# Score tiles kept for the whole run: the next products of a pair's first item wait for that item's top-eight alone, with fewer unread products ahead

## The chip, the cores and the metric

The kernel runs on one core of one Trainium2 chip. The metric is the device time of one execution in microseconds (us). Before the change the median of three runs is 797.43 us (797.13 to 797.91).

## The reference

For 8 batches of 8 heads, with 576 positions and a head size of 64, attention keeps only the 32 largest scores of each row. The result goes through a highway layer with two 512 x 512 weights.

```
scores = scale * np.matmul(q, k.transpose(0, 1, 3, 2))
kth = np.partition(scores, -top_k, axis=-1)[..., -top_k:-top_k + 1]
scores = np.where(scores >= kth, scores, -1e9)
attn = np.exp(scores - max);  attn = attn / (sum + 1e-9)
x = matmul(attn, v)                       # heads side by side: (4608, 512)
H = maximum(x @ w_h, 0);  T = sigmoid(x @ w_t + b_t)
out = T * H + (1 - T) * x
```

## The kernel before

**Units and pairs.** The 576 query rows of a head are four tiles of 128 and a short one of 64. A unit (L59 to L65) is one full query tile of one head, or the short tiles of two heads one above the other in the 128 partitions. Two units make a pair: 288 units, 144 pairs, 18 pairs a batch, of which the last two are the short query tile. An item is one of the two units of a pair; the code calls them s = 0 and s = 1.

**The score tile.** `scores` (L297 to L349) writes the products of query and key of one pair into a tile of three PSUM banks. Item 0 takes bank 0 and the first 64 columns of bank 1, item 1 the last 64 columns of bank 1 and bank 2. For a full query tile four f32 products of 64 rows by 256 columns fill banks 0 and 2 (L311); item 0's operands lie in the partitions 0 to 63, item 1's in 64 to 127. The loop over the two column halves is outside, that over the items inside, so the items alternate. One product with a block-diagonal operand fills both ends in bank 1 (L322). For the short tile each item has four products of 64 x 64 (L328) and two for the ends (L339), item 0 first. The tile comes from a pool of two buffers (L81, L299), so that the products of pair i + 2 wait until every reader of pair i's tile is done.

**What happens to a score tile.** For pair i + 1, DVE finds the eight largest of each of the six 96-wide segments of either item (`segments`, L358, twelve instructions), ACT copies both items to SBUF (L353), and DVE combines the segment lists (`refine`, L375 to L391) into the 24th largest value, a threshold. ACT marks what lies above it with a sign and counts it (`mask_count`, L406, one instruction per item, each followed by a read of the sum). PE adds the marks onto the scores in PSUM (`mask_add`, L419, four products), so that the marked values drop, and DVE takes the top-eight of all 576 columns of each item (`below`, L432, two instructions), which gives the values from rank 25 to 32. From these comes the 32nd value (L438, L448, L451). ACT computes the exponentials (L424); the smaller ones are cut off by a comparison on ACT (L454) or POOL (L457) and a minimum on DVE (L471). A DMA transposes the result (L496), PE multiplies it with the values (L509), and ACT copies a full block of four heads' results out (L523).

**The order of a step.** The order on every engine is written out by hand in `step` (L790 to L908), under a manual schedule. In step i PE's queue takes: the mask additions of pair i (L815); work left from the step before (L824); the values of pair i - 3 (L826), and where these fill a block, the copy on ACT; unread products (`spare`, L829); in some steps a transposition of the next batch's keys or queries (L251); the products of pair i + 2 (L844); a layer's projection (L537 to L551) or a transposition; and four or ten more unread products (L853). DVE takes the segments of pair i + 1, `below` of pair i, `refine` of pair i + 1 and the minimum. Each engine works its queue in order.

**Unread products.** `spare(n)` (L275) issues n bf16 products of 128 x 252 columns into the unused part of the value block's tile; nobody reads them. Ahead of the score products stand 8 of them, or 3 where the pair i + 2 is short and the value block is empty. After a block's copy they write the same single buffer, and so wait for that copy.

`finish` (L965) does the last pair, with the last layers, and takes two more score tiles for them; `begin` (L910) takes one ahead of the first pair.

Of the kernel before, what the change touches and what calls it, by code (L numbers as in the profile page):

```python
# [11 lines left out]
FP32 = mybir.dt.float32  # L12
# [14 lines left out]
def kernel(  # L27
# [10 lines left out]
    nc = tc.nc  # L38
    P = nc.NUM_PARTITIONS
# [7 lines left out]
    nfull = S // P  # L47
# [5 lines left out]
    BANK = 512  # L53
    MAIN = nfull * P
# [4 lines left out]
    units = []  # L59
# [7 lines left out]
    pairs = [(u, u + 1) for u in range(0, NU, 2)]  # L67
    NG = len(pairs)
# [9 lines left out]
    xpool = ctx.enter_context(tc.tile_pool(name="x", bufs=3))  # L78
    fpool = ctx.enter_context(tc.tile_pool(name="f", bufs=2))
    hpool = ctx.enter_context(tc.tile_pool(name="h", bufs=3))  # L80
    xps = ctx.enter_context(tc.tile_pool(name="xps", bufs=2, space=bass.MemoryType.PSUM))  # L81
    ops = ctx.enter_context(tc.tile_pool(name="ops", bufs=1, space=bass.MemoryType.PSUM))
    fps = ctx.enter_context(tc.tile_pool(name="fps", bufs=1, space=bass.MemoryType.PSUM))


    ident_f = consts.tile([P, P], FP32)
# [188 lines left out]
    def spare(n):  # L275
        if "t" not in po:
            po.update(t=pso_tile(), n=0)
        for _ in range(n):
            nc.tensor.matmul(  # L279
                po["t"][:, 4 * DE : BANK],  # L280
                ident_b[:],
                cst[:, 0 : BANK - 4 * DE],
                start=True,
                stop=True,
                skip_group_check=True,
            )
# [7 lines left out]

    def scores(pair, prep):  # L297
        kT, qT, kd = prep
        ps = xps.tile([P, 3 * BANK], FP32, tag="x", name="xs")  # L299
        heads2 = [units[u][2] for u in pair]  # L300
        qt = units[pair[0]][1]
        qs = qt * P
        MB = 2 * BANK
        rest = []
        RA, RB = BANK, 2 * BANK - rem
        if qt < nfull:
            hp = heads2[0][0] // 2
            for n0 in range(0, MAIN, 256):
                for s, mo in ((0, 0), (1, MB)):
                    r = s * D  # L310
                    mm = nc.tensor.matmul(  # L311
                        ps[:, mo + n0 : mo + n0 + 256],
                        qT[r : r + D, hp, qs : qs + P],
                        kT[r : r + D, hp, n0 : n0 + 256],
                        start=(n0 == 0),
                        stop=True,
                        skip_group_check=True,
                    )
                    if s:
                        rest.append(mm)  # L320
            ends = ps[:, BANK:MB].rearrange("p (a n) -> p a n", n=rem)[:, 0 :: BANK // rem - 1, :]
            rest.append(nc.tensor.matmul(ends, qT[:, hp, qs : qs + P], kd[:, hp, :], start=True, stop=True))  # L322
        else:
            for (mo, ro), hh in zip(((0, RA), (MB, RB)), heads2):
                hp = hh[0] // 2
                for n0 in range(0, MAIN, 256):
                    for r in (0, D):
                        mm = nc.tensor.matmul(  # L328
                            ps[r : r + rem, mo + n0 : mo + n0 + 256],
                            qT[r : r + D, hp, qs : qs + rem],  # L330
                            kT[r : r + D, hp, n0 : n0 + 256],
                            start=(n0 == 0),
                            stop=True,
                            skip_group_check=True,
                        )
                        if mo:
                            rest.append(mm)
                for r in (0, D):
                    mm = nc.tensor.matmul(  # L339
                        ps[r : r + rem, ro : ro + rem],  # L340
                        qT[r : r + D, hp, qs : qs + rem],
                        kd[r : r + D, hp, r : r + rem],
                        start=(mo == 0),
                        stop=True,
                        skip_group_check=True,
                    )
                    rest.append(mm)
        both = bass.AP(tensor=ps.tensor, offset=ps[:].offset, ap=[ps[:].ap[0], [3 * BANK - S, 2], [1, S]])
        return ps[:, 0:S], ps[:, 3 * BANK - S : 3 * BANK], both, rest  # L349
# [79 lines left out]
        return [t[:, s, :] for s in range(2)] + [t]  # L429

    def below(u, ps):
        nc.vector.max(wall[:, u, THR + 1 : KTH], ps)  # L432


    def hits(pair):
# [302 lines left out]
    def start_scores(g):  # L738
        b = units[pairs[g][0]][0]
        for u in pairs[g]:  # L740
            for h in units[u][2]:
                ensure_prep(b, h // 2)
        st[g] = dict(ps=scores(pairs[g], preps[b]), sc=[None, None], et=[None, None], e=[None, None])
        st[g]["seg"] = 0
        st[g]["cand"] = cands[g % len(cands)]

# [43 lines left out]
    def step(i):  # L790
# [34 lines left out]
        if back:  # L825
            back_pv(j)  # L826
            back_xs(j)
            st.pop(j)
        spare(8 if i + 2 >= NG or units[pairs[i + 2][0]][1] < nfull or po["n"] else 3)  # L829
        ev = prep_filler() if to_prep and (i <= SPB or (len(to_prep) > 15 - k_in or len(layers) > 2) and i % 2) else None  # L830
        do_work(nc.gpsimd, 2 * dm if prev and not ps_["one"] else dm)
        segs(i + 1, 2 * NSEG)
        if live:
            below(pr[0], st[i]["ps"][0])
            below(pr[1], st[i]["ps"][1])
        if live:
            st[i]["e"] = pair_tile("e")
            expo(pr[0], st[i]["sc"][0], st[i]["e"][0])
# [71 lines left out]
    def begin():  # L910
        done.update((0, hp, part) for hp in range(NP) for part in range(2))
        done.update(((0, 0, 7), (0, 0, 8)))
        piece = partial(prep_piece, stages[0], preps[0])
        dve = nc.vector.tensor_copy
        spare(21)
        xa = xps.tile([P, 3 * BANK], FP32, tag="x", name="xs")
        ev0 = piece(0, 3)
        ev1 = piece(0, 5, xa, dve)
        ev2 = piece(0, 4, po["t"], dve)
        ev1()  # L920
        ev0()
        ev2()
        piece(0, 2, xa[:, BANK : 2 * BANK], dve)()
        po.clear()
        start_scores(0)
        piece(0, 6, pso_tile())()
        evs = [piece(1, 0), piece(1, 5, pso_tile())]
        for ev in evs:
# [36 lines left out]
    def finish():  # L965
# [41 lines left out]
        cur["e"] = pair_tile("e")  # L1007
        for s, u in enumerate(pr):
            expo(u, cur["sc"][s], cur["e"][s])
        x1 = xps.tile([P, 3 * BANK], FP32, tag="x", name="xs")  # L1010
# [10 lines left out]
        x2 = xps.tile([P, 3 * BANK], FP32, tag="x", name="xs")  # L1021
# [141 lines left out]
```

## Time and profile before

| what | value |
|---|---|
| median of three runs | 797.43 us |
| the profiled execution | 797.43 us |
| its span, first to last instruction | 795.7 us |
| PE, DVE, ACT, POOL busy | 693.0, 767.3, 756.3, 564.8 us |
| unread products (L279) on PE | 1,841 rows, 247.1 us |
| mean granted clock of PE | 0.996 |

A row of the profile names line, engine, operation, what it writes and reads, its shape and count; then its busy time, the mean length of one in ns, and the engine's idle time ahead of it with what ended that. Rows overlap where an engine starts an instruction before the last one has ended: the rows of PE give the length from start to modelled end, and products that follow each other start sooner than that. PE is the matrix engine and PEld its weight loads. In the timeline the columns are start, length of the merged rows, engine, line, operation and count.

### The profile page before, as it was taken

Reading aid. Unit: us, or ns where it says so; the run is one execution under the profiler, and the core shown is the slowest. Engines: PE = TensorE matmul, PEld = TensorE weight load, DVE = VectorE, ACT = ScalarE, POOL = GpSimd, SP = SyncE. Lnnn points to the kernel's source line nnn. Section 1 sums busy time; section 2 is a strip of 40 time slices with the busy share of each in tenths; the row PEclk is TensorE's granted clock in tenths of the full one; section 3 lists DMA queues with packets and bytes.
Section 4 is the critical chain, followed back from the end, with each engine's and each line's share of the span. In section 5 each row is a group of like instructions: output and inputs, shape, how many; then the busy total and the mean of one; then the engine's idle time right before and its main releaser. Section 6 shows DMA issues by size and latency. Waiting matters only on the chain.

```text
span 795.7 us, 20350 instructions
## 1 busy us (share of the span) xinstructions
PE 693.0 (87%) x6459; PEld 494.6 (62%) x6459; DVE 767.3 (96%) x3947; ACT 756.3 (95%) x1401; POOL 564.8 (71%) x750
## 2 busy tenths in 40 slices
PE   8889988888988888888997889888998888988884
PEld 6666766566656666566665666656666666666552
DVE  6999999999999999999999999999999999999996
ACT  5999999999999999999999999999999999999984
POOL 2666867877778767787777876788777787776760
PEclk9999999999999999999999999999999999999998
DMA  6699967976899567987689866898677975565643
GB/s 125 88 136 172 127 125 140 159 127 87 140 157 156 104 99 135 159 136 117 106 146 159 133 110 111 154 154 127 107 129 146 162 118 96 97 113 98 114 85 89
DMA packets 341780, 100.32 MB, mean 126 GB/s; under 512 B 326048, under 2 KB 333856, under 8 KB 341664
## 3 DMA queue, kind: packets, MB, share of 16 engines
q1 hardware_dynamic: 286448, 79.14, 52.6%
q0 software_dynamic: 53536, 19.34, 22.5%
q8 instruction: 53, 0.87, 0.4%
q10 hardware_dynamic: 1680, 0.46, 0.3%
q14 instruction: 63, 0.52, 0.2%
HBM read 31.72 MB, written 9.44 MB: 52 GB/s over the span
## 4 chain that ended last, share of the span: by engine, by line
DVE 46%; ACT 32%; PE 16%; issue 2%; DMA 2%; SPq 0%; POOL 0%; DVEq 0%; ACTq 0%; POOLq 0%
DVE cand L358 16%; DVE wall L432 15%; ACT m L406 9%; ACT e L424 8%; ACT sc L353 6%; DVE ep L471 6%; ACT r L454 4%; PE xs L328 4%; PE fp L537 3%; PE pso L279 3%; PE xs L419 2%; PE xs L311 2%; DMA xT<-xb 2%; ACT xs L523 2%; DVE en L382 1%
## 5 line engine op out<-in xcount | busy, mean ns | idle before, releaser
L358 DVE MAX8 cand<-xs 128x8 f32<-128x96 f32 x1728 | 298.0, 252 | 0.4 <-PE xs L311 0.2
L279 PE MATMUL pso<-cst,ident_b 128*128 128x252 bf16 x1841 | 247.1, 272 | 41.8 <-ACT xs L523 39.7
L457 POOL TENSOR_SCALAR r<-sc,wall 128x576 bf16<-128x576 f32 x135 | 232.5, 1722 | 0.0
L424 ACT ACTIVATE e<-sc,be 128x576 bf16<-128x576 f32 x288 | 227.8, 791 | 0.1
L279 PEld LDWEIGHTS <-ident_b 128*128 128x128 bf16 x1841 | 173.5, 98 | 80.7 <-issue 48.9
L432 DVE MAX8 wall<-xs 128x8 f32<-128x576 f32 x288 | 205.2, 756 | 13.3 <-PE xs L419 12.1
L311 PE MATMUL xs<-kT,qT 64*128 64x256 f32 x1024 | 145.3, 400 | 34.0 <-DVE high L375 26.0
L353 ACT COPY sc<-xs 128x1152 f32<-128x1152 f32 x144 | 161.7, 1123 | 0.2
L311 PEld LDWEIGHTS xs<-kT,qT 64*128 64x128 f32 x1024 | 93.0, 186 | 65.5 <-issue 39.3
L406 ACT ACTIVATE m<-xs,wall 128x576 int8<-128x576 f32 x144 | 108.1, 751 | 9.8 <-DVE wall L391 8.6
L471 DVE TENSOR_TENSOR ep<-e,r 128x1024 bf16<-128x1024 bf16 (+2 forms) x236 | 116.4, 493 | 0.3 <-issue 0.2
L448 POOL TENSOR_TENSOR hit<-hit,wall 128x18 f32<-128x18 f32 x143 | 32.1, 225 | 113.5 <-DVE hit L438 113.5
L419 PE MATMUL xs<-m,ident_b 128*128 128x512 bf16 (+1 forms) x576 | 104.7, 285 | 9.0 <-ACT m L406 6.8
L406 ACT ACTIVATE m<-sc,wall 128x576 int8<-128x576 f32 x144 | 112.5, 781 | 0.0
L454 ACT ACTIVATE r<-sc,be 128x576 bf16<-128x576 f32 x143 | 111.0, 776 | 0.0
L509 PEld LDWEIGHTS <-et 128*128 128x128 bf16 (+1 forms) x1600 | 68.6, 100 | 19.9 <-issue 3.5
L400 POOL TENSOR_TENSOR be<-wall,fac 128x4 f32<-128x4 f32 x144 | 29.0, 201 | 71.9 <-DVE ep L471 52.0
L509 PE MATMUL pso<-vb,et 128*128 128x65 bf16 (+1 forms) x1600 | 74.4, 194 | 1.0 <-DMA et<-ep 1.0
L419 PEld LDWEIGHTS <-ident_b 128*128 128x128 bf16 x576 | 51.1, 98 | 35.5 <-issue 13.9
L322 PEld LDWEIGHTS xs<-kd,qT 128*128 128x128 f32 x256 | 38.1, 188 | 42.5 <-issue 42.1
L322 PE MATMUL xs<-kd,qT 128*128 128x128 f32 x256 | 62.5, 326 | 0.0
L625 POOL TENSOR_TENSOR s<-h,x 128x512 f32<-128x512 f32 (+1 forms) x37 | 42.8, 1157 | 1.0 <-ACT h L624 1.0
(128 smaller groups left out, 1005.8 us busy)
## 6 DMA issues: line engine op xcount, KB each, us to landing
kin<-in_k_dram SPq DMA_DIRECT2D x64, 128.0 KB, 3.2
qin<-in_q_dram SPq DMA_DIRECT2D x62, 128.0 KB, 3.1
out_dram<-s SPq DMA_DIRECT2D x30, 256.0 KB, 3.1
s<-h POOLq DMA_DIRECT2D x29, 256.0 KB, 3.8
xb<-x POOLq DMA_DIRECT2D x30, 128.0 KB, 2.7
vb<-in_v_dram POOLq DMA_DIRECT2D x28, 128.0 KB, 3.9
et<-ep SPq DMA_TRANSPOSE x143, 3.9
vb<-in_v_dram POOLq DMA_DIRECT2D x24, 64.0 KB, 3.0
```

The lines of the kernel that those rows point to most:

```text
L279: nc.tensor.matmul(po["t"][:, 4 * DE : BANK], ident_b[:], cst[:, 0 : BANK - 4 * DE], start=True, stop=True, skip_group_check=True,)
L311: mm = nc.tensor.matmul(ps[:, mo + n0 : mo + n0 + 256], qT[r : r + D, hp, qs : qs + P], kT[r : r + D, hp, n0 : n0 + 256], start=(n0 == 0), ...
L353: nc.scalar.copy(sc[:], both)
L358: ins = nc.vector.max(cand[:, s, :], sc[:, s * SEG : (s + 1) * SEG])
L406: nc.scalar.activation(m1[:].bitcast(I8)[:, 1 : 2 * S : 2], ps, AF.Sign, bias=wall[:, u, THR : THR + 1], scale=ABOVE, accum_out=csum[:, u ...
L419: nc.tensor.matmul(ps[:, s0:s1], ident_b[:], m1[:, s0:s1], start=False, stop=True, skip_group_check=True)
L424: nc.scalar.activation(e, sc, AF.Exp, bias=tb(u), scale=scale)
L432: nc.vector.max(wall[:, u, THR + 1 : KTH], ps)
L454: nc.scalar.activation(r, sc, AF.Relu, bias=eb(u), scale=BIGK)
L457: nc.gpsimd.tensor_scalar(r, sc, kth(u), None, ALU.is_ge)
L471: return nc.vector.tensor_tensor(out[:, :, c0:c1], e[:, :, c0:c1], r[:, :, c0:c1], ALU.min)
L509: nc.tensor.matmul(pso[r0 : r0 + ql, col : col + DE], ets[s][:, c, gi * P2 : gi * P2 + ql], vb[:, h, vc, :], start=(c == 0), stop=(c == nc ...
```

## The change

The two score tiles are allocated once and taken in turn (`xss`), instead of from a pool of two. The pool kept all products of pair i + 2 behind all readers of pair i; with kept tiles the order follows from what each product overwrites. `below` now returns its instruction, and `step` keeps that of item 1; `scores` gets the one of two pairs back and declares that item 0's products do not depend on it. So item 0's products wait for item 0's `below` alone, item 1's and the ends' for item 1's too. In the full tiles the loop over items goes outside: both products of item 0, then both of item 1. In the short tiles the order stays. Ahead of the score products stand 3 unread products in every step but the last ones (8). `begin` and `finish` name the tiles that they took from the pool before.

```diff
-    xps = ctx.enter_context(tc.tile_pool(name="xps", bufs=2, space=bass.MemoryType.PSUM))
+    xps = ctx.enter_context(tc.tile_pool(name="xps", bufs=1, space=bass.MemoryType.PSUM))
+    xss = [xps.tile([P, 3 * BANK], FP32, name=f"xs{i}") for i in range(2)]
...
-    def scores(pair, prep):
+    def scores(pair, prep, other=None):
+        def ahead(mm):
+            if other is not None:
+                tc.declare_no_dep(mm.ins, other.ins, reason="another bank")
+
-        ps = xps.tile([P, 3 * BANK], FP32, tag="x", name="xs")
+        ps = xss[pair[0] // 2 % 2]
...
-            for n0 in range(0, MAIN, 256):
-                for s, mo in ((0, 0), (1, MB)):
+            for s, mo in ((0, 0), (1, MB)):
+                for n0 in range(0, MAIN, 256):
...
                     if s:
                         rest.append(mm)
+                    else:
+                        ahead(mm)
...
                         if mo:
                             rest.append(mm)
+                        else:
+                            ahead(mm)
...
     def below(u, ps):
-        nc.vector.max(wall[:, u, THR + 1 : KTH], ps)
+        return nc.vector.max(wall[:, u, THR + 1 : KTH], ps)
...
-        st[g] = dict(ps=scores(pairs[g], preps[b]), sc=[None, None], et=[None, None], e=[None, None])
+        st[g] = dict(ps=scores(pairs[g], preps[b], st[g - 2]["below"] if g > 1 else None), sc=[None, None], et=[None, None], e=[None, None])
...
-        spare(8 if i + 2 >= NG or units[pairs[i + 2][0]][1] < nfull or po["n"] else 3)
+        spare(8 if i + 2 >= NG else 3)
...
             below(pr[0], st[i]["ps"][0])
-            below(pr[1], st[i]["ps"][1])
+            st[i]["below"] = below(pr[1], st[i]["ps"][1])
```

In `begin` and `finish` the calls for a new tile become `xss[1]`, `xss[i % 2 ^ 1]` and `xss[i % 2]`.

More of the change, by code (lines that the diff above doesn't have):

```diff
@@ L915, in begin @@
         spare(21)
-        xa = xps.tile([P, 3 * BANK], FP32, tag="x", name="xs")
+        xa = xss[1]
         ev0 = piece(0, 3)
@@ L1009, in finish @@
             expo(u, cur["sc"][s], cur["e"][s])
-        x1 = xps.tile([P, 3 * BANK], FP32, tag="x", name="xs")
+        x1 = xss[i % 2 ^ 1]
         project(bank(x1, 1), z["qt"], z["xT"], wt, True)
@@ L1020, in finish @@
         pick_b(pr, hit)
-        x2 = xps.tile([P, 3 * BANK], FP32, tag="x", name="xs")
+        x2 = xss[i % 2]
         cur["et"] = halves(et_tile())
```

## The prediction

> **What bounds the kernel now.** I read the page first: the busy shares, then the costliest groups.
>
> ```profile
> PE 693.0 (87%) x6459; PEld 494.6 (62%) x6459; DVE 767.3 (96%) x3947; ACT 756.3 (95%) x1401; POOL 564.8 (71%) x750
> ```
> ```profile
> L358 DVE MAX8 cand<-xs 128x8 f32<-128x96 f32 x1728 | 298.0, 252 | 0.4 <-PE xs L311 0.2
> L279 PE MATMUL pso<-cst,ident_b 128*128 128x252 bf16 x1841 | 247.1, 272 | 41.8 <-ACT xs L523 39.7
> ...
> L432 DVE MAX8 wall<-xs 128x8 f32<-128x576 f32 x288 | 205.2, 756 | 13.3 <-PE xs L419 12.1
> L311 PE MATMUL xs<-kT,qT 64*128 64x256 f32 x1024 | 145.3, 400 | 34.0 <-DVE high L375 26.0
> ```
>
> DVE is busy for 767.3 of 795.7 us and ACT for 756.3, so either engine bounds most steps and only their idle time can be won. The segment top-eights (L358), which read the score tiles that this change makes ready sooner, wait 0.4 us in the whole run: they are never late. The only DVE wait of size stands ahead of the full top-eight (L432), 13.3 us, and it is for the mask additions on PE (L419). PE's own waits for DVE ahead of the score products (L311, 34.0 us idle) and ahead of the fillers (L279, 41.8 us) cost nothing unless something behind them is late. Next I read the waits of DVE and of ACT, each by itself.
>
> ```profile
> DVE wall L432 <- PE xs L419: 12.1, 25, 1.1
> ```
> ```profile
> ACT m L406 <- DVE wall L391: 8.6, 23, 0.9
> ACT xs L523 <- PE pso L509: 6.8, 12, 1.1
> ```
>
> So PE holds DVE up 25 times and ACT (the copy of a value block, L523) 12 times. Where? The last two pairs of each batch, the short query tile, are eight places; the waits in a window around the first of them and around the last are these (DVE, ACT, DVE, ACT):
>
> ```profile
> DVE wall L432 <- PE xs L419: 1.1, 2, 0.7
> ```
> ```profile
> ACT xs L523 <- PE pso L509: 0.5, 1, 0.5
> ```
> ```profile
> DVE wall L432 <- PE xs L419: 0.7, 1, 0.7
> DVE wall L432 <- PE pso L509: 0.7, 1, 0.7
> ```
> ```profile
> ACT m L406 <- DVE wall L391: 0.9, 1, 0.9
> ACT xs L523 <- PE pso L509: 0.6, 1, 0.6
> ```
>
> Over the eight windows DVE waits 8.0 us for L419 (six of 1.1, two of 0.7), two thirds of 12.1, and ACT waits 4.6 us for L509 (two of 0.5, six of 0.6). The timeline of PE in the fourth of them shows why.
>
> ```profile
> 376.05 0.48 PE L279 MATMUL pso<-cst,ident_b 128*128 128x252 bf16 x3 [0.70 <-ACT xs L523]
> 376.71 1.08 PE L328 MATMUL xs<-kT,qT 64*64 64x256 f32 x8 [0.17 <-DVE wall L432]
> ...
> 380.92 1.02 PE L279 MATMUL pso<-cst,ident_b 128*128 128x252 bf16 x8
> 381.78 0.60 PE L251 MATMUL fp<-ident_f,qin 128*128 128x128 f32 x4
> 382.46 1.08 PE L328 MATMUL xs<-kT,qT 64*64 64x256 f32 x8
> ...
> 384.56 1.04 PE L537 MATMUL fp<-wt,xT 128*128 128x512 bf16 x4
> ...
> 386.08 0.65 PE L419 MATMUL xs<-m,ident_b 128*128 128x512 bf16 x4
> ```
> ```profile
> 380.88 1.43 DVE L432 MAX8 wall<-xs 128x8 f32<-128x576 f32 x2 [0.35 <-PE xs L419]
> ...
> 386.84 1.43 DVE L432 MAX8 wall<-xs 128x8 f32<-128x576 f32 x2 [0.72 <-PE xs L419]
> ```
> ```profile
> 384.97 0.32 ACT L406 ACTIVATION_READ_ACCUMULATOR m<-sc,wall 128x1 f32 x1
> ...
> 387.09 0.38 ACT L523 COPY xs<-pso 128x260 f32<-128x260 f32 x1 [0.64 <-PE pso L509]
> ```
>
> From 376.71 to 386.57 PE shows no wait at all: eight fillers at 380.92, a transposition, the score products of the second short pair at 382.46, a projection, fillers, and the mask additions at 386.08, though the masks are ready when ACT reads its second sum, at 384.97 + 0.32 = 385.29. PE is the bound here; DVE loses 0.35 and then 0.72, ACT 0.64.
>
> **The change part by part.** *Fillers, 8 to 3.* They go ahead of every pair's products but the last two and those that had 3 already: 1,171 unread products are built instead of 1,841, so 670, or 134 times five. One costs PE (1.02 - 0.27) / 7 = 0.107 us, by the row of 380.92 (first start to last start, one product's 0.27 off), five 0.54 us, and all 72 us. In an ordinary step this is hidden:
>
> ```profile
> 301.99 1.02 PE L279 MATMUL pso<-cst,ident_b 128*128 128x252 bf16 x8 [0.46 <-ACT xs L523]
> 302.94 1.13 PE L311 MATMUL xs<-kT,qT 64*128 64x256 f32 x8
> 304.00 0.49 PE L322 MATMUL xs<-kd,qT 128*128 128x128 f32 x2
> 304.33 1.24 PE L279 MATMUL pso<-cst,ident_b 128*128 128x252 bf16 x10
> 305.40 0.82 PE L419 MATMUL xs<-m,ident_b 128*128 128x512 bf16 x4
> ```
> ```profile
> 301.32 1.43 DVE L432 MAX8 wall<-xs 128x8 f32<-128x576 f32 x2
> ```
>
> Here the products may begin when the second L432 ends, 301.32 + 1.43 = 302.75, and they begin at 302.94; without five fillers PE would reach them at 302.40 and wait.
>
> *The start, item by item.* Item 0's two products (four passes on PE) now wait for the first L432 only. The second starts 1.43 - 0.76 = 0.67 us after the first, so item 0 can start 0.67 us sooner. Item 1's products wait for the second L432 as the whole block did, and the product of the key ends (L322) stands behind them. In the ordinary step item 1 thus starts at 302.75 at the earliest instead of 302.94, the block ends at most 0.19 us sooner, and behind it nothing was late: L358 never waits and the L432 of this step shows no idle time. Worth: 0. For the short pairs the order within an item is unchanged, and the second item's products stand behind the first's, so the whole block moves up with its start.
>
> *The order, item 0 first, then item 1.* Before, the products of the two items alternate. Each f32 product is two passes (1,024 rows at L311 for 128 pairs of four products). Three narrow cuts of PE's timeline through one block:
>
> ```profile
> 302.94 0.49 PE L311 MATMUL xs<-kT,qT 64*128 64x256 f32 x2
> ```
> ```profile
> 303.26 0.38 PE L311 MATMUL xs<-kT,qT 64*128 64x256 f32 x2
> ```
> ```profile
> 303.48 0.38 PE L311 MATMUL xs<-kT,qT 64*128 64x256 f32 x2
> ```
>
> Passes come in pairs that run together, 0.22 us apart. Two passes of one product use the same 64 rows of the array; so the pair at 302.94 is item 0's first pass and item 1's first, and item 1's did not wait for item 0's second, which stands ahead of it in the program. The two halves of the array run as two streams. I take it that this holds in the new order too: item 1's stream starts when its wait ends, whatever remains of item 0's. Cost 0. The bounds: if nothing overlaps, eight passes at 0.22 take 1.76 instead of 0.88, 0.88 us more for each of 128 blocks, of which the earlier start takes back 0.67 or the fillers 0.54. The nearest row, the pair of passes, says 0.
>
> The Trainium skill, "TensorE: Matmul & The Clock Gate", Part 3, says that matmuls stay in program order, "strict FIFO, no reordering". By that rule item 1 would stand behind item 0's four passes, and the time would be that of the first rival below. The pair at 302.94 speaks against it.
>
> *The new sign from the first L432.* DVE now tells PE once more per pair, 142 times. Between 0 and the row's own rounding, 0.02 us each: 0 to 2.8 us; I take 0. The instructions on DVE, ACT, POOL and SP and their order are as before; the static tiles take the turns that the pool gave, so no other wait is added.
>
> *The sum.* In the window of 376 to 387 the first short block starts 0.17 us sooner (PE's idle time there was for L432); it has three fillers before and after. The second gets this and five fillers, 0.17 + 0.54 = 0.71 us: it starts at 381.75, and the first L432 has ended by then, at 380.88 + 0.76 - 0.17 = 381.47. That takes ACT's 0.64 whole and DVE's 0.72 but for 0.01; the additions come at 385.37, just behind the masks' 385.29. What counts is the smaller, ACT's. Over eight batches 4.6 us. DVE is then some 0.1 us ahead of ACT (0.72 and part of 0.35 against 0.64), and wins part of it back where ACT waits for DVE (8.6 us at L406): 8 times 0.06, 0.5 us. In the last batch DVE waits twice 0.7 us: 0.5 us more. The other 12.1 - 8.0 = 4.1 us of L432's waits hold some that hang on a DMA for a projection:
>
> ```profile
> PE fp L537 <- DMA xT<-xb: 2.6, 3, 1.1
> ```
>
> Three, of up to 1.1 us, which nothing here moves: 2.6 us stay at most, and of the 1.5 left I count a third, where fillers made PE late: 0.5 us. Sum 4.6 + 0.5 + 0.5 + 0.5 = 6.1 us. The profiled execution took 797.43 us, 1.7 of it around the span, and that is also the median of the three runs. Forecast **791.3 us**; with every small term at nothing 792.8, with DVE's 8.0 us taken whole and the 1.5 too 787.9.
>
> **Rivals.** *Strict order on PE (slower).* Item 1 runs behind item 0's four passes: in a block gated by L432 the end comes 0.88 - 0.67 = 0.21 us later, in one gated by fillers 0.34. It decides where the mask additions come from PE just in time; ACT's masks hold them up in only 26 of 144 steps:
>
> ```profile
> PE xs L419 <- ACT m L406: 6.8, 26, 0.7
> ```
>
> In the other 118, PE's arrival sets them; with cover in half (the step at 305.40 has 0.3 us), 59 x 0.21 = 12.4 us are lost. The point is 6.1 / 0.21 = 29 exposed steps: above it the change loses. Time 797.4 - 6.1 + 12.4 = 803.7. Chance 0.06.
>
> *The clock falls (slower).* Fillers keep PE busy, and the granted clock is 1.00 in the cuts of the middle:
>
> ```profile
> 182.00:185.50 3.50, 2.27 (x24) 1.34 (x21) 3.50 (x16) 3.50 (x9) 3.13 (x3) 1.00 0.91 134
> 300.00:312.00 12.00, 10.59 (x101) 7.40 (x100) 11.76 (x63) 11.47 (x22) 8.46 (x11) 1.00 0.87 136
> ```
>
> A step takes 795.7 / 144 = 5.5 us. An ordinary stretch is busy for 0.88 and would be for about 0.78 (0.54 us less a step); the emptiest is at 0.65 and could go to 0.50, which no row shows at a full clock. If the clock halved once a batch for a step, PE's 0.78 x 5.5 = 4.3 us would take 8.6, 3.1 more than the step has: 8 x 3.1 = 25 us, 816. Chance 0.04.
>
> *ACT takes over.* ACT is busy for 95%. If its masks hold the additions of the freed step up (they are ready only 0.08 us ahead of the 385.37 above), or if its work, not DVE's, sets the steps after, a quarter of the 6.1 us is won, 1.5: 796.0. Chance 0.14.
>
> *More than the sum.* Ordinary steps with small hidden waits for PE gain as well, up to the 787.9 above: 788.5. Chance 0.12.
>
> *The forecast*, 791.3, between 789.5 and 794: chance 0.64. That the change does not do what it says I leave at nothing: in the built program item 0's first product waits for one DVE sign less than item 1's.
>
> **The numbers.** A measurement of this kernel can tell about 0.2%, 1.6 us, from no change. The range runs from 788.5, the larger gain, to 796.0, where ACT takes over; the two slower rivals, 0.10, and the outer tails of the others are left out. Faster by over 0.2%: 0.64 + 0.12 + 0.05 of ACT's case = 0.81; within: 0.09 of it; slower: 0.06 + 0.04 = 0.10.
>
> **What would show it.** Right: at the short pairs L432's wait falls from 1.1 us a batch to below 0.4, and ACT's at L523 from 0.6 to near 0; L279 has 1,171 rows; item 0's products begin within 0.2 us of the first L432's end, and item 1's passes run beside what is left of item 0's or at the second L432's end; L358 still shows no wait. Wrong: L311's block gets longer by 0.4 us or more counted from the second L432's end, waits at L419 in ordinary steps grow, the granted clock shows under 1.00 before 780 us, or ACT's wait at L406 grows by what L523 loses.

## The result, and the profile after

The changed kernel took 787.9 us (median of four runs, 787.44 to 789.91) beside 797.63 us for the kernel before (four runs); the ratio is 0.9881, with a 95% interval of 0.9867 to 0.9895. It is faster, as forecast, but by 9.7 us instead of 6.1. Eleven later runs of the same kernel (below) took 788.6 to 793.4; the median of all fifteen is 790.35 us. So two questions were open: what made the gain larger than the sum, and why the same kernel differs by 6 us (787.4 to 793.4) from run to run.

The profiled execution took 787.89 us, its span is 786.2 us, the mean granted clock 0.996. First the page: busy shares and groups, with busy time, mean ns, idle time ahead and what ended it.

```profile
PE 683.7 (87%) x5709; PEld 481.4 (61%) x5789; DVE 764.9 (97%) x3947; ACT 753.2 (96%) x1401; POOL 565.8 (72%) x750
...
L316 PE MATMUL xs<-kT,qT 64*128 64x256 f32 x1024 | 209.1, 402 | 21.3 <-DVE wall L441 18.9
...
L441 DVE MAX8 wall<-xs 128x8 f32<-128x576 f32 x288 | 203.8, 747 | 6.3 <-PE xs L428 2.8
...
L280 PE MATMUL pso<-cst,ident_b 128*128 128x252 bf16 x1171 | 174.7, 273 | 43.0 <-ACT xs L532 40.7
```

1,171 unread products (L280) cost 174.7 us, 72.4 less, and PE still holds its share, since the score products (L316) now begin early and wait for the second top-eight within their block. The full top-eight (L441, then L432) has 6.3 us of idle time ahead of it in place of 13.3. The waits of the trace (engine and line waited for, us, times, longest):

```profile
PE xs L428 <- ACT m L415: 15.6, 59, 0.7
...
DVE wall L441 <- PE xs L428: 2.8, 6, 0.9
...
ACT xs L532 <- PE pso L518: 2.2, 4, 1.1
```

DVE's wait for the mask additions fell from 12.1 to 2.8, ACT's for the value block from 6.8 to 2.2, and PE now waits for the masks 59 times instead of 26: at most of the short pairs PE is no longer the late one. The fifth batch's short pairs show it. Before, on PE, on DVE and on ACT (start, length):

```profile
472.97 1.08 PE L328 MATMUL xs<-kT,qT 64*64 64x256 f32 x8 [0.40 <-DVE wall L432]
...
477.19 1.02 PE L279 MATMUL pso<-cst,ident_b 128*128 128x252 bf16 x8
...
478.72 1.08 PE L328 MATMUL xs<-kT,qT 64*64 64x256 f32 x8
...
482.34 0.65 PE L419 MATMUL xs<-m,ident_b 128*128 128x512 bf16 x4
```
```profile
477.14 1.43 DVE L432 MAX8 wall<-xs 128x8 f32<-128x576 f32 x2 [0.35 <-PE xs L419]
...
483.10 1.43 DVE L432 MAX8 wall<-xs 128x8 f32<-128x576 f32 x2 [0.72 <-PE xs L419]
```
```profile
471.66 0.38 ACT L523 COPY xs<-pso 128x260 f32<-128x260 f32 x1
...
477.56 1.13 ACT L353 COPY sc<-xs 128x1152 f32<-128x1152 f32 x1
478.68 0.59 ACT L252 COPY qT<-fp 128x512 f32<-128x512 f32 x1
...
481.32 0.76 ACT L454 ACTIVATE r<-sc,be 128x576 bf16<-128x576 f32 x1
482.11 0.60 ACT L648 ACTIVATE tt<-fp 128x512 f32<-128x512 f32 x1
483.35 0.38 ACT L523 COPY xs<-pso 128x260 f32<-128x260 f32 x1 [0.64 <-PE pso L509]
```

The same place in the changed kernel, again PE, DVE, ACT:

```profile
471.31 0.48 PE L280 MATMUL pso<-cst,ident_b 128*128 128x252 bf16 x3
...
472.26 1.08 PE L335 MATMUL xs<-kT,qT 64*64 64x256 f32 x8
...
475.88 0.65 PE L428 MATMUL xs<-m,ident_b 128*128 128x512 bf16 x4
```
```profile
471.30 1.41 DVE L441 MAX8 wall<-xs 128x8 f32<-128x576 f32 x2
476.64 1.43 DVE L441 MAX8 wall<-xs 128x8 f32<-128x576 f32 x2
481.80 1.41 DVE L441 MAX8 wall<-xs 128x8 f32<-128x576 f32 x2
```
```profile
466.25 0.38 ACT L532 COPY xs<-pso 128x260 f32<-128x260 f32 x1
...
472.16 1.13 ACT L362 COPY sc<-xs 128x1152 f32<-128x1152 f32 x1
473.15 0.62 ACT L253 COPY qT<-fp 128x512 f32<-128x512 f32 x1
...
475.79 0.81 ACT L463 ACTIVATE r<-sc,be 128x576 bf16<-128x576 f32 x1
476.45 0.63 ACT L657 ACTIVATE tt<-fp 128x512 f32<-128x512 f32 x1
476.93 0.41 ACT L532 COPY xs<-pso 128x260 f32<-128x260 f32 x1
```

No wait is left on DVE or ACT. From the first short pair's full top-eight to the second's it was 483.10 - 477.14 = 5.96 us and is 476.64 - 471.30 = 5.34. From one value block's copy to the next ACT took 483.35 - 471.66 = 11.69 us and takes 476.93 - 466.25 = 10.68: 1.01 less, though its idle column had shown 0.64.

Laying the two profiled executions side by side, by the start of each step's segment top-eights (L358, L367), the gain of 9.44 us (their ends included) falls into four parts:

| part | gain, us |
|---|---|
| eight places with the short pairs: 0.42, 1.09, 0.73, 0.73, 1.06, 1.07, 1.06, 0.80 | 6.96 |
| ordinary steps between them, net | 1.38 |
| before the first step | 0.43 |
| behind the last step | 0.67 |

### The profile page after: what moved, and what is told of

It is laid out like the page before. It is cut to its first block, busy times and chain, and to the rows that moved or that the text cites. A ratio compares the mean times of both kernels' runs of the same rounds, so it can differ in the third digit from the quotient of the medians.

```text
span 786.2 us, 18861 instructions
## 1 busy us (share of the span) xinstructions
PE 683.7 (87%) x5709; PEld 481.4 (61%) x5789; DVE 764.9 (97%) x3947; ACT 753.2 (96%) x1401; POOL 565.8 (72%) x750
## 3 DMA queue, kind: packets, MB, share of 16 engines
HBM read 31.72 MB, written 9.44 MB: 52 GB/s over the span
## 4 chain that ended last, share of the span: by engine, by line
DVE 43%; ACT 41%; PE 11%; issue 3%; DMA 2%; SPq 0%; POOL 0%; another core or an unknown queue 0%; DVEq 0%; ACTq 0%; POOLq 0%
DVE cand L367 15%; ACT m L415 12%; DVE wall L441 12%; ACT e L433 10%; ACT sc L362 8%; DVE ep L480 6%; ACT r L463 5%; PE pso L280 2%; PE xs L335 2%; DMA xT<-xb 2%; PE fp L546 2%; DVE en L391 2%; DVE en L394 1%; ACT xs L532 1%; ACT kT L253 1%
## 5 line engine op out<-in xcount | busy, mean ns | idle before, releaser
L367 DVE MAX8 cand<-xs 128x8 f32<-128x96 f32 x1728 | 297.4, 246 | 0.3 <-PE xs L316 0.2
L433 ACT ACTIVATE e<-sc,be 128x576 bf16<-128x576 f32 x288 | 230.6, 801 | 0.1
L316 PE MATMUL xs<-kT,qT 64*128 64x256 f32 x1024 | 209.1, 402 | 21.3 <-DVE wall L441 18.9
L280 PE MATMUL pso<-cst,ident_b 128*128 128x252 bf16 x1171 | 174.7, 273 | 43.0 <-ACT xs L532 40.7
L441 DVE MAX8 wall<-xs 128x8 f32<-128x576 f32 x288 | 203.8, 747 | 6.3 <-PE xs L428 2.8
L316 PEld LDWEIGHTS xs<-kT,qT 64*128 64x128 f32 x1024 | 146.6, 186 | 61.8 <-DVE wall L441 40.6
L280 PEld LDWEIGHTS <-ident_b 128*128 128x128 bf16 x1171 | 108.1, 98 | 75.0 <-issue 49.8
L428 PE MATMUL xs<-m,ident_b 128*128 128x64 bf16 (+1 forms) x522 | 97.5, 275 | 16.9 <-ACT m L415 15.6
L428 PEld LDWEIGHTS <-ident_b 128*128 128x128 bf16 x576 | 53.0, 97 | 47.3 <-issue 25.0
```

Of the source, the lines that this page charges most:

```text
L280: nc.tensor.matmul(po["t"][:, 4 * DE : BANK], ident_b[:], cst[:, 0 : BANK - 4 * DE], start=True, stop=True, skip_group_check=True,)
L316: mm = nc.tensor.matmul(ps[:, mo + n0 : mo + n0 + 256], qT[r : r + D, hp, qs : qs + P], kT[r : r + D, hp, n0 : n0 + 256], start=(n0 == 0), ...
L367: ins = nc.vector.max(cand[:, s, :], sc[:, s * SEG : (s + 1) * SEG])
L428: nc.tensor.matmul(ps[:, s0:s1], ident_b[:], m1[:, s0:s1], start=False, stop=True, skip_group_check=True)
L433: nc.scalar.activation(e, sc, AF.Exp, bias=tb(u), scale=scale)
L441: return nc.vector.max(wall[:, u, THR + 1 : KTH], ps)
```

## The experiments

Ratios stand against runs of the kernel before on the same chip, whose medians were 797.77, 798.01, 797.78 and 797.53 us in the four groups of runs. Gains of single steps are worked out as in the table.

### Which part of the change does it

**Fewer unread products alone.** The kernel before, with 8 -> 3.

```diff
-        spare(8 if i + 2 >= NG or units[pairs[i + 2][0]][1] < nfull or po["n"] else 3)
+        spare(8 if i + 2 >= NG else 3)
```

> The kernel before with 3 unread products ahead instead of 8, nothing else. Theory W (the gain is made where PE alone sets the end, at the two short pairs of each batch, and there the start behind the first top-eight and the five fillers each free PE only as far as the other allows): in the trace of before the second short pair's products start 0.15 us after the second top-eight's end, as do those of most steps, so with the old wait five fillers less free almost nothing there; about 796.5, between 795.5 and 797.2. Rival F (PE's time is what counts, so 5 x 0.107 us less per step do it alone): 788 to 790. Rival S (the earlier start alone does it): 797.6.

Measured: 796.52 us (795.72 to 803.06), ratio 0.9998 (0.9981 to 1.0015). Neither short pair gained more than 0.06 us in any batch. Without an earlier start PE reaches the products sooner and then waits for the second top-eight. The other steps of the profile gained 1.4 us, as with the whole change, and the median is 1.25 us lower than before; three of the twelve runs, at a mean clock of 0.988 to 0.991, took 799 to 803 us and bring the ratio, which is one of means, to 1.

**The early start alone.** The changed kernel with the old line for the unread products.

> The changed kernel with the 8 unread products of before: only the start item by item and the order are new. Theory W: the first short pair of a batch starts 0.1 to 0.6 us sooner, since it has 3 fillers in both, and the top-eight after it loses its wait of 0.35 us (0.46 with the overlap of 0.09 that it usually has); the second short pair keeps its wait of 0.72 us, since PE works without a gap from the first to it. About 795, between 794 and 796. Rival F: 797.6. Rival S: 788 to 789.

Measured: 795.17 us (793.93 to 795.49), ratio 0.9961 (0.9949 to 0.9974). In most batches the first short pair gained 0.12 to 0.46, as with the whole change, and the second 0.07 to 0.16 (0.50 to 0.62 with the whole change); in the third batch the second gained 0.52 of 0.73. The eight places together gained 3.5 us. With eight products in the way PE reaches the second pair's block late whatever may start early.

**The early start in the short pairs alone**, with three unread products:

```diff
                     if s:
                         rest.append(mm)
-                    else:
-                        ahead(mm)
```

> The changed kernel, but in the full query tiles item 0's products wait for both top-eights again; in the short tiles they wait for item 0's alone. Theory W: the full tiles' early start is worth nothing by itself, as item 1's products and the ends' set the block's end; 787.9 to 788.9. Rival S (the early start counts in all steps, 126 of 142 are full): 7/8 of the gain is lost, 796. Rival F: 787.9.

Measured: 791.26 us (788.29 to 794.75), ratio 0.9923 (0.9899 to 0.9948). The short pairs gained as with the whole change, step by step within 0.04.

**The early start in the full tiles alone**, the same cut in the other branch.

> The changed kernel, but in the short tiles item 0's products wait for both top-eights again, and only the full tiles start early. Theory W: the short pairs lose what the early start gives there, up to 0.6 us at the first and up to 0.6 at the second, most of a gain of 0.7 to 1.1 us a batch; 794 to 796. Rival S: 789. Rival F: 787.9.

Measured: 796.15 us (793.91 to 799.97), ratio 0.9972 (0.996 to 0.9984); the first short pair gained nothing, the second 0.10 in most batches and the last batch 0.35, 1.0 us in all.

So the 7 us need two things at once and at one place: the start by item and at most three unread products, both at the short pairs. Apart they bring 0.2 and 3.5 us there. In full tiles the early start is worth nothing that can be measured.

### Which engine sets the freed steps

The prediction counted what ACT showed as idle, the smaller of two figures. Two loads test it: one copy of 128x512, read by nobody, in the step behind the short pairs of every batch, once on ACT and once on DVE.

```diff
             copy_both(i + 1)
+        if k_in == 16:
+            nc.scalar.copy(idle_o[:], idle_i[:])
```

> The changed kernel with one more ACT copy of 128x512 f32 (0.6 us, some 0.5 from start to start) in each of the eight batches, in the step in which ACT stood idle for 0.64 us ahead of L523, behind the score copy; its result isn't read. Theory W (DVE's work sets the steps, ACT lags and catches up in ordinary steps, where its instructions take about 0.6 us less than DVE's): the time grows by 0 to 1.5 us, 788 to 789.5. Rival A, the prediction's own (ACT's idle time caps what a batch gains): 8 x 0.5 = 4 us, 792.

Measured: 794.09 us (792.51 to 800.23), ratio 0.997 (0.9952 to 0.9988), 3.1 us above the changed kernel on the same chip. ACT and DVE of this run in the fifth batch:

```profile
482.28 0.68 ACT L851 COPY idle_o<-idle_i 128x512 f32<-128x512 f32 x1
482.80 0.83 ACT L433 ACTIVATE e<-sc,be 128x576 bf16<-128x576 f32 x1
```
```profile
480.06 1.43 DVE L441 MAX8 wall<-xs 128x8 f32<-128x576 f32 x2
485.66 1.43 DVE L441 MAX8 wall<-xs 128x8 f32<-128x576 f32 x2 [0.36 <-PE xs L428]
```

The copy takes 0.52 us of ACT (482.28 to 482.80), and six of the eight batches lost 0.47 to 0.51 us by it (the fourth 0.22, the last nothing). DVE's next full top-eight comes 5.60 us after the last one instead of 5.16, and waits, since the masks are late. ACT has no room here.

The same copy on DVE (`nc.vector.tensor_copy`):

> The changed kernel with one copy of 128x512 on DVE, read by nobody, in the step behind the two short pairs of each batch, where the same copy on ACT cost its whole 0.48 us a batch. Theory ACT (ACT alone sets these steps, DVE has the 0.4 us to spare that it waited more than ACT): nothing to 0.15 us a batch, the time of the changed kernel within 1 us. Rival both (DVE and ACT had lost the same 1.0 us a batch to the late additions, ACT part of it hidden in the overlap of its rows): most of the copy, 0.25 us or more a batch, 2 us or more in all.

Measured: 792.02 us (790.26 to 794.45), ratio 0.9929 (0.9911 to 0.9946), 1.25 us above the changed kernel on the same chip. DVE in the fifth batch:

```profile
480.86 1.43 DVE L441 MAX8 wall<-xs 128x8 f32<-128x576 f32 x2
482.21 0.41 DVE L851 COPY idle_o<-idle_i 128x512 f32<-128x512 f32 x1
486.35 1.41 DVE L441 MAX8 wall<-xs 128x8 f32<-128x576 f32 x2
```

From top-eight to top-eight it is 5.49 us instead of 5.16: 0.33 is lost, all that the copy holds DVE for (its next row starts at 482.53, 0.32 later). So it is in six batches, 0.33 or 0.34; the fourth lost 0.08. So DVE has no room either, and the reading by which it had 0.4 us to spare falls: both engines had lost the same to the late additions. The total rose by less than the 2 us expected; in the profile later steps give a part back: three that lose 0.25, 0.31 and 0.33 us in the changed kernel lose nothing in this run.

The fourth batch is the exception in both runs: there ACT and DVE each had 0.25 us to spare. A run below without unread products at this place shows who held it up.

### Why the changed kernel's time differs from run to run

**The changed kernel again**, twice, on two more chips.

> The changed kernel as it is, once more beside the three others. Each theory expects 787.9, and steps in which a projection waits for a DMA to come and go by up to 1 us from run to run.

Measured: 791.03 us (788.58 to 793.4), ratio 0.9919 (0.9906 to 0.9933).

> The changed kernel as it is, a third time. Theory clock (its runs differ by the number of 3.4 us stretches at half clock that they happen to get): time falls as the granted clock rises, runs at 0.996 take 787.4 to 788.5 us, each 0.001 less adds about 1 us, median 788 to 791.5. Rival (the spread comes from elsewhere, transfers above all): no relation between clock and time among the runs.

Measured: 790.77 us (789.08 to 793.43), ratio 0.9913 (0.9897 to 0.993). The profiled run took 792.39, 4.5 us more than the first profile, and at the short pairs it gained the same to within 0.02 us. What differs is 3.76 us in the first five steps, 1.34 us in step 81 and, the other way, 0.79 us in step 117. Of the 3.76, 2.14 are lost ahead of the first step. PE's timeline there, in this run and in the first profile:

```profile
7.07 0.66 PE L252 MATMUL fp<-ident_f,kin 128*128 128x128 f32 x2 [0.64 <-DMA kin<-in_k_dram]
...
9.23 1.84 PE L316 MATMUL xs<-kT,qT 64*128 64x256 f32 x8
```
```profile
6.07 0.41 PE L252 MATMUL fp<-ident_f,kin 128*128 128x128 f32 x2
...
7.83 1.13 PE L316 MATMUL xs<-kT,qT 64*128 64x256 f32 x8
```

The first load comes 1.0 us later, and the same block of eight products takes 1.84 us instead of 1.13. The clock had not risen yet: the trace's record of the full clock begins at 10.71 us in this run and at 5.68 in the first profile, and the next such block, at 13.10, takes 1.14. The other 1.62 us are a fall of the clock. Stretches of both runs (bounds and length, busy time of PE, PEld, DVE, ACT, POOL, then the granted clock, the DMA share and GB/s):

```profile
21.00:24.30 3.30, 1.55 (x13) 1.15 (x14) 2.98 (x17) 3.30 (x6) 2.14 (x3) 1.00 0.35 22
24.50:27.70 3.20, 3.20 (x16) 2.05 (x13) 2.43 (x13) 2.84 (x7) 2.60 (x3) 0.50 0.99 117
```
```profile
19.40:22.70 3.30, 1.64 (x15) 1.19 (x13) 3.22 (x15) 3.30 (x6) 2.14 (x4) 1.00 0.22 18
22.80:26.10 3.30, 2.97 (x24) 2.37 (x24) 3.15 (x14) 3.30 (x7) 2.17 (x3) 1.00 1.09 139
```

PE was busy for 1.55 of 3.30 us and then had half its clock for 3.4 us: its two steps lost 1.78 us, where the first profile lost 0.16, with 1.64 of 3.30 at the same place and the clock kept. The difference in step 81 is a transfer. PE waits for it in the profile of before and in this run, and not at all in the first profile of the changed kernel, which waits at another place:

```profile
433.17 1.04 PE L537 MATMUL fp<-wh,xT 128*128 128x512 bf16 x4 [1.14 <-DMA xT<-xb]
```
```profile
433.08 1.04 PE L546 MATMUL fp<-wh,xT 128*128 128x512 bf16 x4 [1.44 <-DMA xT<-xb]
```
```profile
616.80 1.04 PE L546 MATMUL fp<-wh,xT 128*128 128x512 bf16 x4 [1.21 <-DMA xT<-xb]
```

So the expectation that clock alone makes the spread is half right. In this group the two runs at clock 0.997 were the shortest (789.08 and 789.5), but the four at 0.993 to 0.995 lie between 790.51 and 793.43 without order. Over more runs the link is plainer. Of all fifteen runs of the changed kernel the five at 0.996 or 0.997 took 787.4 to 789.5 us, the ten below 788.6 to 793.4. Of the twelve with fewer unread products alone, nine at 0.993 or above took 795.7 to 797.6 and the three below 799.1 to 803.1.

### What the unread products are for

**None ahead of the score products**, `spare(8 if i + 2 >= NG else 0)`:

> The changed kernel with no unread products ahead of the score products at all, instead of 3. Theory W: at the short pairs PE is 3 x 0.107 us sooner, and the first short pair no longer waits for ACT's copy L532; of the 0.13 + 0.14 us that DVE still waits there (0.22 each with the overlap) up to 0.2 each are won, 0 to 3 us in all, 785 to 788; ACT's masks are ready only 0.15 to 0.24 us before the additions then, which caps it. Rival C (the fillers hold the clock): the granted clock falls below 0.99 and the time is above 790.

Measured: 797.25 us (793.36 to 803.86), ratio 0.9998 (0.9977 to 1.0019), mean clock 0.984 in the profile and 0.966 to 0.984 over the runs. All of the gain is gone, though in the profile the short pairs gain 6.97 us as before: the other steps lose 6.32. Six stretches of 3.4 us ran at half clock, and the steps at each lost 0.9 to 1.7 us against the first profile; one from the middle, and the stretch ahead of it:

```profile
417.90:421.20 3.30, 2.39 (x19) 1.70 (x15) 3.30 (x18) 3.30 (x7) 2.52 (x4) 1.00 0.89 157
421.40:424.60 3.20, 2.93 (x22) 1.87 (x21) 2.78 (x15) 3.16 (x8) 3.17 (x4) 0.50 1.03 127
```

**None around the short pairs alone**, three elsewhere:

```diff
+        spare(8 if i + 2 >= NG else 0 if k_in in (14, 15, 16) else 3)
...
+        spare(0 if k_in in (14, 15) else 4 if late else 10)
```

> The changed kernel without any unread products in the steps that issue the two short pairs' products, none ahead of them (nor in the step behind) and none ahead of the next mask additions; the other steps keep 3 and 4 or 10. Theory W: like the one without fillers ahead, and 4 x 0.107 us more at the additions, but ACT's masks cap it at some 0.2 us for each of 16 pairs: 785 to 787.5. Rival C: as above. Rival F: 8 x 2 x 0.43 to 0.75 = 7 to 12 us less, 776 to 781.

Measured: 792.38 us (790.5 to 794.3), ratio 0.9927 (0.9913 to 0.9942). In the fifth to seventh batch the pairs gained 0.45 and 0.77 and lost 0.11 in the next step, so there PE's last 0.1 us is not the limit any more. In the fourth they gained 0.45 and 0.45, 0.17 more than with the changed kernel, and lost nothing behind: there PE still was the late one, which is why a load on ACT or DVE cost less. Three stretches ran at half clock, and the total is 1.35 us above the changed kernel's on the same chip.

**None in the steps at all**, neither there nor ahead of the mask additions:

> The changed kernel with no unread products in the steps at all, neither ahead of the score products nor ahead of the mask additions (those of the start, the finish and the last two steps stay). Theory clock (fillers earn their place by holding the granted clock): the clock falls in many stretches of 3.4 us, mean granted clock below 0.98, and with 0.6 to 1.2 us lost in each the time is above 797 us. Rival (fillers are dead weight on PE, the clock needs few of them): clock above 0.99 and 788 us or less.

Measured: 821.01 us (814.58 to 826.29), ratio 1.0283 (1.0245 to 1.032). A long stretch of this run and of the first profile:

```profile
60.00:420.00 360.00, 297.19 (x2095) 196.34 (x2093) 344.39 (x1777) 343.26 (x637) 262.56 (x341) 0.88 0.77 128
```
```profile
60.00:420.00 360.00, 318.06 (x2673) 223.05 (x2710) 356.10 (x1845) 355.13 (x663) 274.17 (x355) 1.00 0.81 134
```

With the fillers gone the clock is 0.88 in place of 1.00 (0.865 over the run), PE does less in the same time, and DVE and ACT lose some 12 us each in this stretch alone (344.39 and 343.26 busy of 360, against 356.10 and 355.13). The unread products pay for themselves by the clock.

**Eight in full tiles, three at the short pairs.** If only the short pairs gain, the other fillers could stay and hold the clock:

```diff
+        spare(8 if i + 2 >= NG or units[pairs[i + 2][0]][1] < nfull else 3)
```

> The changed kernel, with eight unread products again ahead of the products of full tiles and three only ahead of the two short pairs of each batch. Theory S (all of the gain sits at the short pairs, where the start by item and the five fillers fewer are both needed; the other 500 or so fillers that the change left out cost nothing where they stood, and hold the clock up): 788 to 790 us, as fast as the changed kernel's quick runs, its runs within about 2 us of each other, granted clock 0.996 or more in the profile and no stretch below 1.00 before 770 us. Theory F (eight fillers in the way of full tiles cost time also in ordinary steps): 792 to 795 us.

Measured: 791.84 us (790.16 to 792.73), ratio 0.9923 (0.991 to 0.9936): between the two theories, and both have a share. This version has 630 more unread products than the changed kernel. The short pairs gained as before but for 0.26 us in the second batch, the clock stayed full up to 774.6 us, and the five runs differ by 2.6 us (4.8 and 4.4 in the two repetitions above). But two steps with a projection lost 0.96 and 0.60 us, which lost 0.10 and nothing with three products, several others were 0.1 to 0.3 longer than with three, and the finish is 2.0 us longer. In the two steps and in the finish PE waits for a transfer (the second step's wait is 0.54 us), here and, in the finish, in the first profile:

```profile
235.61 1.04 PE L546 MATMUL fp<-wh,xT 128*128 128x512 bf16 x4 [1.07 <-DMA xT<-xb]
...
773.95 0.89 PE L518 MATMUL pso<-vb,et 128*64 128x65 bf16 x20 [2.11 <-DMA et<-ep]
```
```profile
770.98 0.83 PE L518 MATMUL pso<-vb,et 128*64 128x65 bf16 x20 [1.06 <-DMA et<-ep]
```

So the fillers' own price is the 0.1 to 0.3 of some steps. The larger losses stand at waits for transfers, and they are not the luck of one run: the profiles of the next two versions, also with eight, wait at the same places (0.58 and 0.72 us, 0.53 and 0.56 us, in the finish 2.42 and 2.26), while the changed kernel waits in neither step in any of its three profiles, and 1.02 to 1.06 us in the finish. In turn all three versions miss the wait of 1.0 to 1.3 us at 307 to 311 us that the changed kernel's profiles have. How the products move these transfers is not shown. Two variants of it: the early start only at the short pairs, and the items alternating again in full tiles.

> As the run with eight fillers in full tiles, but item 0 starts behind its own top-eight in the short pairs alone; in full tiles all products wait for the second full top-eight. Theory S: within 1 us of that run, since the early start in full tiles hides no wait. Rival (the early start in full tiles is worth something, in the steps where a projection stands ahead of the mask additions): 1.5 to 3 us slower.

Measured: 792.26 us (789.72 to 793.08), ratio 0.9924 (0.9911 to 0.9936).

> As the run with eight fillers in full tiles, but the products of the two items alternate again in full tiles (the order of before). Theory two streams (the two halves of the array run on their own, so the order between the items has no price): within 1 us of that run. Rival (order matters, item by item lets item 0's segment top-eights or item 0's passes go ahead): 1 to 3 us slower.

Measured: 791.72 us (790.51 to 792.25), ratio 0.992 (0.9907 to 0.9932). The three agree within 0.6 us: neither the early start in full tiles nor the order of the items has a price or a worth there that can be measured.

**Five in full tiles:** `spare(8 if i + 2 >= NG else 5 if units[pairs[i + 2][0]][1] < nfull else 3)`.

> The changed kernel with five unread products ahead of the products of full tiles, three ahead of the short pairs. Theory clock: two more fillers a step hold the clock up and still cost less in the steps with a projection than eight do: no stretch of halved clock before 770 us, 788 to 790 us, runs within 2.5 us of each other. Rival (fillers in full tiles cost, the clock is no matter): between the changed kernel and the run with eight, 790 to 792 us.

Measured: 790.17 us (788.97 to 791.94), ratio 0.9912 (0.9897 to 0.9926), beside 790.77 for the changed kernel on the same chip. The clock held up to 772.5 us, and the finish waits 1.91 us for its transfer, as with eight. The difference cannot be told from none; no version here beats the changed kernel by a measurable amount.

## Why the prediction was right in kind and short in size

**Fillers 8 to 3: right.** 670 fewer, 72.4 us less on PE, no gain at the short pairs by themselves. The ordinary steps hide them only nearly: with eight in full tiles some steps were 0.1 to 0.3 us longer.

**The start, item by item: right.** Worth nothing in full tiles, needed in the short ones. The prediction adds its 0.17 to the fillers' 0.54 and does not say that the two come only together; the runs show it: in the fourth batch 0.28 and 0.00 us apart, 0.73 together.

**The order of the items: right, cost 0.** The first rival, strict order on PE, is refuted by the equal times with and without it, and by the length of a block that starts with both items released:

```profile
310.95 1.14 PE L316 MATMUL xs<-kT,qT 64*128 64x256 f32 x8
```

1.14 us, as the 1.13 of before; strict order would have added 0.88. In the trace its eight passes start in pairs 0.01 us apart. So on PE "each engine works its queue in order" holds for either half of the array by itself. The Trainium skill's rule ("TensorE: Matmul & The Clock Gate", Part 3) that matmuls stay in program order does not hold here for products on two halves of the array.

**DVE's extra sign: 0 fits.** L441 took 203.8 us, L432 had 205.2.

**The failed step is the sum: "What counts is the smaller, ACT's. Over eight batches 4.6 us."** With its two additions for the same places it gave 5.6 us; they brought 6.96. Two things were wrong in it: the one place that it was worked out from, and the wait of ACT that it took for the limit there.

*One window stood for eight.* In the fourth batch, from which it was worked out, the forecast per batch was 0.64 + 0.06 = 0.70, and 0.73 came. There the first short block could start only 0.17 us sooner. In the fifth the row of 472.97 has 0.40 in its place, the first pair gained 0.46 instead of 0.23, and the batch 1.06; three others came to between 1.06 and 1.09. ACT's idle time ahead of L523 was 0.64 in the fourth to the seventh batch alike, so it cannot be what tells 0.73 from 1.06. What PE was freed by can: 0.17 + 0.54 = 0.71 in the fourth, which PE alone held up, and 0.40 + 0.54 = 0.94 in the fifth to seventh, 0.1 less than they gained. That the fourth came out near the forecast was luck: ACT's 0.64 stands close to PE's 0.71.

*ACT's idle column is not what ACT lost.* Its rows normally overlap: 475.79 + 0.81 is 0.15 past the next start, 476.45. A wait shorter than this leaves no idle time, and a longer one shows that much less. By starts, before against after, the fifth batch lost 478.68 - 477.56 = 1.12 against 0.99, 482.11 - 481.32 = 0.79 against 0.66, and 483.35 - 482.11 = 1.24 against 0.48: 0.13 + 0.13 + 0.76 = 1.02, the 1.06 gained but for 0.04. The idle column has 0.64 of it. In the fourth batch ACT by the same starts had lost 0.12 + 0.72 = 0.84, more than the 0.73 that came. The Trainium skill, "Perfetto Trace Analysis", section "Optimizing Scalar/DVE Operations", says that the half of an operation's access overhead in which the write is acknowledged overlaps with the next instruction. This trace agrees that rows overlap, by 0.15 us. That ACT leaves no room beyond the gain stood the test outside the fourth batch (0.47 lost to a load of 0.52); DVE, loaded, had no room either. So "the smaller" chose between two readings of one loss.

**The small terms.** The third "of the 1.5 left" was 0.5 for all other steps; they brought 1.38 in the first profile, 0.79 and -0.90 in the two repetitions. The three waits for a transfer, "which nothing here moves", did move: that of 1.14 at 433.17 vanished (1.21 us gained in its step), and one of 1.21 at 616.80 appeared (0.79 lost). Start and finish, 1.1 us together in the first profile, were not in the sum. The finish is 0.6 to 0.7 us shorter in all three profiles and belongs to the change. The start and the other steps belong to the run as much as to the change: in the second repetition's profile the first five steps are 3.76 us worse, and the span shrank by 5.0 in all, while the short pairs gained 6.95.

**How much of the miss is luck.** The median of the first four runs lies 0.6 us below the range's lower end of 788.5; that of all fifteen, 790.35, lies inside it, 1.0 us below the forecast. In every profile of the changed kernel the short pairs' term is too small by 1.3 to 1.4 us and the finish brings 0.6 to 0.7 that was in no term; the start, the transfers and the clock of a run take part of this back or add to it. That "DVE's 8.0 us taken whole and the 1.5 too" gives 787.9 to the digit is chance as well: the parts were 6.96, 1.38 and 1.10.

**"ACT takes over"** did not happen on the whole: PE waits for the masks oftener (15.6 us, 59 times). In two steps of the first batch, though, PE waits 0.35 us for them, DVE then 0.41 and 0.35 us ahead of L441, and the steps lose 0.19 and 0.30 us. **"The clock falls"** is real, with its price overestimated: not 3.1 us a time but 1.2 and 1.6 in the two profiles of the changed kernel that have one (in the first repetition's a stretch at half clock, from 699.6 us, lost 1.22; that of 24.5 us above cost 1.6), and 0.8 to 1.7 in the two runs with none ahead (nine stretches). With three products the changed kernel stands near that edge: two of its three profiles have such a stretch before 780 us, and that sign, named as one that would show the prediction wrong, came without undoing the gain.

What stays open: why a stretch with PE busy for half of it lowers the clock in one run and not in another, and how the spread of 787.4 to 793.4 us divides between clock and transfers: the clock has a clear share, but only single runs have a trace.

## What to carry to other kernels

A gain that hangs on one late engine is read from starts, from the same row of one step to that of the next, in every place where it occurs; the idle column leaves out waits shorter than the usual overlap of rows, and one place is no pattern for eight. Two small edits can be worth 0.2 and 3.5 us apart and 7 together, when each alone leaves the other's wait as the last one. Before work without a reader is removed from PE, look at the granted clock with that work gone.

## What the runs showed of the hardware

The granted clock falls for one stretch of 3.41 us to 0.50 and returns by itself. In the run with no products ahead the six falls begin at 21.89, 120.88, 421.25, 510.00, 605.57 and 748.93 us: 29, 88, 26, 28 and 42 times 3.413 us apart, so they stand on a grid of that length. A fall came after a stretch in which PE was busy for 0.47 of the time (21.0 to 24.3 us in the second repetition) or for 0.72 (2.39 of 3.30, from 417.9 us, with no products ahead). The Trainium skill, "TensorE: Matmul & The Clock Gate", Part 1, has a free-running window of 3.4 us and a fall after an idle one; the length and the grid agree, but here no stretch was idle, and 0.50 of the time (1.64 of 3.30) once passed without a fall.

Work that comes some 4 us sooner can miss a wait for a transfer altogether or meet a new one: single steps moved by +1.21 and -0.79 us in one profile, and in a later one of the same kernel by neither.
